# Last-query value product of two head pairs on 64-column halves of TensorE, with one division for both, in a fused attention and gated-MLP kernel

## The chip, the cores and the metric

The kernel runs on one core of one Trainium2 chip. The metric is device time in microseconds (us). Three runs gave 441.95, 442.55 and 442.66 us; the median is 442.55 us.

The engines of the core are named as the profile names them: PE is TensorE's matmul side, PEld its weight load side, DVE is VectorE, ACT is ScalarE, POOL is GpSimd and SP is the queue that issues most of the DMAs. PSUM is the memory that TensorE writes its products to, SBUF the memory that it reads from.

## What is computed

A threshold attention feeds a gated MLP with a spatial mixing step. Batch 8, 8 heads, 576 positions, head dimension 64.

```python
scores = (q @ k.T) / 8                        # per batch and head, 576 x 576
keep   = scores >= rowmax(scores) - tau       # tau = 0.02
attn   = where(keep, exp(scores - rowmax), 0); attn /= attn.sum(-1)
x      = concat_heads(attn @ v)               # 8 x 576 x 512
h = relu(x @ w_in); u, v = halves(h)          # 512 columns each
v = layernorm(v); v = w_spatial @ v + b_spatial
out = (u * v) @ w_out
```

The part that the change touches is `attn @ v`, with its division by the row sum, for the last 64 of the 576 queries of each head.

## The kernel before, in words

**Tiles.** Heads are handled as 32 pairs (`NPAIR`), four pairs to a batch. A pair's 576 queries are four chunks of 128 (chunk c of `steps`, c from 0 to 3) and a rest of 64. The rests of two neighbouring pairs, 2m and 2m+1, are put together into one chunk of 128 rows (chunk 4): rows 0 to 63 are those of pair 2m, rows 64 to 127 those of pair 2m+1. A step computes the scores of one chunk for both heads of the pair (L712, 64x64 tiles of TensorE), the row maxima (L746 on DVE), the exponentials (L761 or L764 on ACT, then L776 on DVE or L781 on ACT) and leaves bf16 numerators.

**The transposed numerators.** For the value product the numerators must lie with keys on the partitions and queries on the free axis. They are transposed by DMA (`turn_p`, L787; `turn_rest`, L799) or, for some rests, by TensorE (`pr_pe`). For the rests of pairs 2m and 2m+1 the result is a tile `ptr` of 128 x 9 x 128: nine blocks of 128 keys, and in each block 128 query columns, of which the first 64 belong to pair 2m and the last 64 to pair 2m+1. Blocks 0 to 3 are the first head's keys, blocks 5 to 8 the second head's, block 4 holds the last 64 keys of both heads.

**The value product.** `weigh` (L390) makes the product of one such tile with one pair's values. It issues nine matmuls: one with block 4 and 130 moving columns (L392; 2 heads x (64 values + 1 column of ones)), and eight with 65 moving columns (L397). The stationary side is always a full 128-column block of the transposed tile, and the column of ones makes the row sum come out as column 64 of each head. `pv` (L411) calls `weigh` for two chunks of one pair, `pv_rest` (L446) calls it for the two pairs that share a rest tile: pair 2m's values with all 128 query columns into PSUM columns 0 to 129, then pair 2m+1's values with all 128 query columns into columns 130 to 259. Of the first product only partitions 0 to 63 are used, of the second only 64 to 127; the other half of each is computed and never read.

**The division.** `divide` (L400) takes the reciprocals of the row sums of a PSUM tile (L404: 128 x 4 values) and multiplies (L406). For `pv` that is one multiplication of 128 x 256. For `pv_rest` it is two, of 64 x 128 each: the partitions of each pair with that pair's columns. The result goes to `xn`, block 8.

**What sets the order.** Every engine's instructions are issued in the order that the strings `ORDER` (L16 to L82) spell out by hand, one token for each small task; the same string serves every batch from the fourth on. `R0` and `R1` are the matmuls of `pv_rest` for the two rest tiles of a batch, `r0` and `r1` their divisions; both of a batch's rests come after its chunk 4 scores, `R1` in the following batch's string. `P`/`p` are `pv`, `S`/`Y` scores (L712), `M` maxima (L746), `QR` (L357) and `QA`/`QB` (L338) the f32 transposes of queries and keys, `u` (L610 and, for its last part, L615), `v`, `s` (L639) and `o` (L668) the MLP. After the strings, the last rest's product is issued by hand among the last MLP tasks (L1079).

**Buffers that bind neighbours.** Products other than scores go through `bank()` (L291), which has only two PSUM banks (`ps_f`, `bufs=2`) until the last stretch. A task's matmuls can start only when the division or copy of the task two banks earlier has been done. Scores have two buffers of their own.

**64-column stationary tiles** occur in the kernel already: `ends` (L526) puts two products into partitions 0 to 63 and 64 to 127 of one bank with 64 stationary columns each (L530, L533), alternating between them. In the profile their shape is written 128*64; full blocks are 128*128 and the scores 64*64.

Of the kernel before, what the change touches and what calls it, by code (L numbers as in the profile page):

```python
# [11 lines left out]
ALU = mybir.AluOpType  # L12
# [75 lines left out]
def kernel(  # L88
# [17 lines left out]
    nc = tc.nc  # L106
# [6 lines left out]
    P = 128  # L113
# [29 lines left out]
    v_ring = [const.tile([P, 10, D + 1], BF16, name=f"v{i}") for i in range(4)]  # L143
# [147 lines left out]
    def bank(dtype=F32, n=512):  # L291
        if wide:

            turn[0] += 1
            if turn[0] % 8 not in (2, 3):
                return wide[0].tile([P, n], dtype, name="t")
        return ps_f.tile([P, n], dtype, name="f")
# [5 lines left out]
    qks, pts, xns, xts = {}, {}, {}, {}  # L303
# [83 lines left out]
            turn(tm, P * (c - 1), 0, c)  # L387
        nc.scalar.mul(out=qkt[:, 0, 192:576], in_=tm[:, 0:384], mul=scale)

    def weigh(t, at, pt, vt):  # L390

        nc.tensor.matmul(out=t[:, at:at + 130], lhsT=pt[:, 4, :],  # L392
                         rhs=vt[:, 4:6, :].rearrange("p b d -> p (b d)"),
                         start=True, stop=False)
        for h in range(2):
            for j in range(4):
                nc.tensor.matmul(out=t[:, at + 65 * h:at + 65 * h + 65], lhsT=pt[:, 5 * h + j, :],  # L397
                                 rhs=vt[:, 6 * h + j, :], start=False, stop=(h == 1 and j == 3))

    def divide(t, parts):  # L400

        o = t[:, 0:260].rearrange("p (g d) -> p g d", d=65)
        r = small.tile([P, 4], F32, name="r")
        nc.vector.reciprocal(out=r, in_=o[:, :, 64])  # L404
        for ps, g0, g1, dst in parts:
            nc.vector.tensor_tensor(  # L406
                out=dst, in0=o[ps, g0:g1, 0:64],
                in1=r[ps, g0:g1].unsqueeze(2).broadcast_to([ps.stop - ps.start, g1 - g0, 64]),
                op=ALU.mult)

    def pv(i, part):  # L411

        b, hp = divmod(i, HP)
        hold = {}

        def mm():
            t = hold["t"] = bank()
            for k in range(2):
                weigh(t, 130 * k, pts[i, part][:, k], v_ring[i % 4])

        def ev():
            xn = x_nat(i // 2)
            at = 4 * (i % 2) + 2 * part
            divide(hold["t"], [(slice(0, P), 0, 4,
                                xn[:, at:at + 2, :].rearrange("p c (h d) -> p (c h) d", h=2))])
        return "dve", mm, ev

    def xt_of(b):
# [5 lines left out]
    def x_nat(m):  # L434

        if m not in xns:
            xns[m] = xp.tile([P, 9, P], BF16, name="xn")
        return xns[m]
# [7 lines left out]
    def pv_rest(m):  # L446

        hold = {}

        def mm():  # L450
            t = hold["t"] = bank()
            for k in range(2):
                weigh(t, 130 * k, pts[m], v_ring[(2 * m + k) % 4])

        def ev():
            xn = x_nat(m)[:, 8, :]
            divide(hold["t"], [(slice(64 * k, 64 * k + 64), 2 * k, 2 * k + 2,
                                xn[64 * k:64 * k + 64].rearrange("p (h d) -> p h d", h=2))
                               for k in range(2)])
        return "dve", mm, ev  # L460

    def x_of(b, f, cols):
# [225 lines left out]
        return "act", mm, ev, send  # L688


    halves = [slice(64 * k, 64 * k + 64) for k in range(2)]
    at = (96, 864)

    def on_act(g):
# [322 lines left out]
    with tc.manual_schedule():  # L1017
# [18 lines left out]
        for _ in range(7):  # L1036
            nc.tensor.matmul(out=ps_f.tile([P, 512], F32, name="f").rearrange(
                "p (a b) -> p a b", a=4), lhsT=warm,
                rhs=warm.unsqueeze(1).broadcast_to([P, 4, P]), start=True, stop=True)
# [84 lines left out]
```

## Time and profile before

| what | value |
|---|---|
| median of three runs | 442.55 us |
| lowest and highest run | 441.95 and 442.66 us |
| profiled execution, first to last instruction (span) | 440.2 us |
| median run less that span (what lies around it) | 2.35 us |
| instructions of the program | 12827 |
| mean granted TensorE clock | 0.999 |
| busy in the batch from 242.5 to 293.0 us: PE, DVE, ACT, POOL | 49.74, 47.10, 47.73, 21.71 of 50.50 us |
| waits of DVE for scores, whole span | 9.3 us (22 times) and 8.5 us (16 times) |
| `pv_rest` in the span | 16 times, 18 matmuls and 3 DVE instructions each |

How to read it: the page gives a busy time for each engine, a chain of work that is followed back from the last instruction, and groups of instructions with their mean durations. Matmuls overlap, so 49.74 us of PE busy time do not mean that TensorE had no room left; the distance from the start of one matmul to the start of the next is what a product really occupies. A table by stage shows the batches from 192 us to 394 us to be nearly equal, 50.5 us each. In a timeline row, the first number is the start and the second the length of a run of like instructions.

### The profile page before, as it was taken

The numbers are of one execution on the slowest core, as the hardware profiler recorded it, in microseconds if no ns is written. First come the engines' busy times: TensorE is split into PE (matmuls) and PEld (weight loads), VectorE is DVE, ScalarE is ACT, GpSimd is POOL, SyncE is SP. The second block draws the span as 40 slices with busy tenths as digits, with TensorE's granted clock in tenths as the row PEclk, the third lists the DMA queues.
The fourth block names the chain that finished last, engine by engine and source line by source line (L and its number), as shares of the span: only waits on it lengthen the run. The fifth ranks groups of instructions, "written<-read, shape, count | busy, mean of one in ns | idle before, by whom it ended". The sixth has DMA issues, their size and how long they took to land.

```text
span 440.2 us, 12827 instructions
## 1 busy us (share of the span) xinstructions
PE 411.0 (93%) x4997; PEld 260.9 (59%) x5048; DVE 394.3 (90%) x641; ACT 388.0 (88%) x621; POOL 178.7 (41%) x383
## 2 busy tenths in 40 slices
PE   8677789999999999999999999999999999999995
PEld 4454556566555666666565666666566666565553
DVE  6997899998999898999999998999989998999782
ACT  3899799999899999999999989999899999999352
POOL 1445443860416511773146711574127711345021
PEclk9999999999999999999999999999999999999999
DMA  7999999899999999999999999999999998976913
GB/s 197 284 213 215 286 224 240 176 180 208 247 157 246 189 188 193 223 220 187 234 216 166 246 216 200 221 231 182 218 188 221 235 190 158 163 111 83 281 67 109
DMA packets 222620, 88.15 MB, mean 200 GB/s; under 512 B 193632, under 2 KB 218336, under 8 KB 222560
## 3 DMA queue, kind: packets, MB, share of 16 engines
q1 hardware_dynamic: 222032, 86.48, 95.0%
q8 instruction: 40, 0.66, 0.6%
q0 software_dynamic: 160, 0.52, 0.3%
q10 hardware_dynamic: 368, 0.33, 0.2%
q14 instruction: 20, 0.16, 0.1%
HBM read 32.79 MB, written 9.44 MB: 96 GB/s over the span
## 4 chain that ended last, share of the span: by engine, by line
DVE 36%; PE 35%; ACT 18%; issue 8%; DMA 1%; POOL 0%; POOLq 0%; DVEq 0%; ACTq 0%
PE s L712 14%; DVE s L746 13%; DVE p L776 9%; DVE negm L746 6%; ACT e L761 6%; ACT e L764 4%; ACT p L781 4%; PE f L610 3%; PE f L668 3%; PE f L397 2%; PE f L639 2%; DVE xn L406 2%; PE f L338 2%; DVE st L565 2%; PE f L545 2%
## 5 line engine op out<-in xcount | busy, mean ns | idle before, releaser
L712 PE MATMUL s<-qkT 64*64 64x160 f32 (+1 forms) x2304 | 171.8, 415 | 13.5 <-ACT e L761 7.3
L712 PEld LDWEIGHTS s<-qkT 64*64 64x64 f32 x2304 | 106.7, 132 | 68.4 <-ACT e L761 17.4
L761 ACT ACTIVATE e<-s,negm 128x576 f32<-128x576 f32 x168 | 117.2, 744 | 12.1 <-DVE negm L752 6.5
L746 DVE TENSOR_REDUCE s<-s 128x2 f32<-128x1152 f32 (+1 forms) x91 | 115.3, 1268 | 10.8 <-PE s L712 9.3
L764 ACT ACTIVATE e<-s,negm 128x576 f32<-128x576 f32 x120 | 84.8, 749 | 9.4 <-DVE negm L746 8.1
L746 DVE TENSOR_REDUCE negm<-s 128x2 f32<-128x1152 f32 (+1 forms) x62 | 81.2, 1313 | 8.8 <-PE s L712 8.5
L776 DVE SCALAR_TENSOR_TENSOR p<-e,ctau 128x1152 bf16<-128x1152 f32 x60 | 85.5, 1427 | 1.3 <-ACT e L764 1.2
L781 ACT ACTIVATE p<-e 128x1152 bf16<-128x1152 f32 x68 | 79.0, 1171 | 0.4
L197 POOL COPY qn<-ql 128x512 f32<-128x512 f32 x31 | 25.5, 821 | 81.1 <-PE s L712 80.7
L397 PE MATMUL f<-v,pT 128*128 128x65 bf16 x1008 | 44.5, 194 | 0.0
L397 PEld LDWEIGHTS <-pT 128*128 128x128 bf16 x1024 | 41.4, 97 | 3.5 <-issue 1.8
L350 POOL COPY qkT<-qkT 64x64 f32<-64x64 f32 x32 | 7.9, 247 | 85.3 <-PE s L712 42.4
L406 DVE TENSOR_TENSOR xn<-f,r 128x256 bf16<-128x256 f32 (+1 forms) x93 | 35.4, 380 | 2.9
L639 PE MATMUL f<-wsT,vn 128*128 128x512 bf16 x117 | 32.6, 380 | 1.4 <-ACT qkT L320 0.4
L610 PE MATMUL f<-xT,w_in 128*128 128x512 bf16 x111 | 29.4, 381 | 0.5
L392 PE MATMUL f<-v,pT 128*128 128x130 bf16 x126 | 27.7, 220 | 1.1 <-DVE xT L314 0.7
L595 POOL TENSOR_SCALAR vn<-vrel,rs,nm 128x512 bf16<-128x512 f32 (+1 forms) x35 | 27.0, 770 | 3.6
L320 ACT COPY qkT<-f 128x512 f32<-128x512 f32 (+1 forms) x56 | 24.5, 439 | 3.4 <-PE f L357 3.2
L545 PE MATMUL f<-w_in,xT 128*128 128x512 bf16 x99 | 26.8, 379 | 0.8
L668 PE MATMUL f<-w_o,gT 128*128 128x512 bf16 x92 | 24.2, 380 | 0.4
L224 POOL CAST v<-vl 128x512 bf16<-128x512 f32 x32 | 20.0, 625 | 10.3 <-PE s L712 9.4
L230 POOL CAST v<-vx 64x64 bf16<-64x64 f32 x64 | 20.8, 326 | 1.9
(166 smaller groups left out, 570.9 us busy)
## 6 DMA issues: line engine op xcount, KB each, us to landing
vl<-in_v_dram SPq DMA_DIRECT2D x16, 512.0 KB, 4.7
ql<-in_q_dram SPq DMA_DIRECT2D x15, 512.0 KB, 5.0
kl<-in_k_dram SPq DMA_DIRECT2D x15, 512.0 KB, 5.3
out_dram<-oo SPq DMA_DIRECT2D x12, 512.0 KB, 5.0
uT<-in_moe_w_in_dram SPq DMA_DIRECT2D x3, 512.0 KB, 4.8
uT<-in_moe_w_spatial_dram SPq DMA_DIRECT2D x2, 576.0 KB, 4.6
pT<-p SPq DMA_TRANSPOSE x65, 6.3
vx<-in_v_dram SPq DMA_DIRECT2D x16, 64.0 KB, 3.7
```

The costliest lines, as they stand in the source:

```text
L397: nc.tensor.matmul(out=t[:, at + 65 * h:at + 65 * h + 65], lhsT=pt[:, 5 * h + j, :], rhs=vt[:, 6 * h + j, :], start=False, stop=(h == 1 an ...
L406: nc.vector.tensor_tensor(out=dst, in0=o[ps, g0:g1, 0:64], in1=r[ps, g0:g1].unsqueeze(2).broadcast_to([ps.stop - ps.start, g1 - g0, 64]), ...
L545: nc.tensor.matmul(out=t, lhsT=x_of(b, f, slice(c * P, (c + 1) * P)), rhs=w_in[:, f, 512:1024], start=(f == 0), stop=(f == 3))
L610: nc.tensor.matmul(out=t, lhsT=w_in[:, m, f * P:(f + 1) * P], rhs=x_of(b, m, slice(0, 512)), start=(m == 0), stop=(m == 3))
L639: nc.tensor.matmul(out=t, lhsT=vn[:, c, f * P:(f + 1) * P], rhs=wsT[:, c, 0:512], start=(c == 0), stop=(c == 4))
L668: nc.tensor.matmul(out=t[:n], lhsT=gs[b][:, f, c * P:c * P + n], rhs=w_o[:, f, :], start=(f == 0), stop=(f == 3))
L712: made.append(nc.tensor.matmul(out=s_ring[g % 2][halves[k], at[h] + lo:at[h] + hi], lhsT=qks[n][halves[h], 0, m:m + 64], rhs=qks[n][halves ...
L746: nc.vector.tensor_reduce(out=nm[:, heads], in_=view(s_ring[g % 2], at[h0], dims), axis=AX.X, op=ALU.max, negate=True)
L761: nc.scalar.activation(out=e, in_=s, func=ACT.Prelu, bias=bias_, scale=scale if steps[g][1] == 4 else 1.0, alpha=1e30)
L764: nc.scalar.activation(out=e, in_=s, func=ACT.Exp, bias=bias_)
L776: nc.vector.scalar_tensor_tensor(out=numerators(g), in0=ef, scalar=ctau, in1=ef, op0=ALU.is_ge, op1=ALU.mult)
L781: nc.scalar.activation(out=numerators(g), in_=e_ring[g % 3].rearrange("p h s -> p (h s)"), func=ACT.Exp)
```

## The change

`weigh` gets a parameter `rows`, by default all 128. It selects the stationary columns of the transposed tile and the partitions of the PSUM tile. `pv_rest` passes columns 0 to 63 for pair 2m and 64 to 127 for pair 2m+1, and both write to the same PSUM columns, 0 to 129. The four groups of 65 columns become two, and one division of 128 x 128 serves both pairs in place of two of 64 x 128. `pv` computes what it did.

```diff
-    def weigh(t, at, pt, vt):
-        nc.tensor.matmul(out=t[:, at:at + 130], lhsT=pt[:, 4, :],
+    halves = [slice(64 * k, 64 * k + 64) for k in range(2)]
+    def weigh(t, at, pt, vt, rows=slice(0, P)):
+        t = t[rows]
+        nc.tensor.matmul(out=t[:, at:at + 130], lhsT=pt[:, 4, rows],
                          rhs=vt[:, 4:6, :].rearrange("p b d -> p (b d)"),
                          start=True, stop=False)
         for h in range(2):
             for j in range(4):
-                nc.tensor.matmul(out=t[:, at + 65 * h:at + 65 * h + 65], lhsT=pt[:, 5 * h + j, :],
-                                 rhs=vt[:, 6 * h + j, :], start=False, stop=(h == 1 and j == 3))
-    def divide(t, parts):
-        o = t[:, 0:260].rearrange("p (g d) -> p g d", d=65)
+                nc.tensor.matmul(out=t[:, at + 65 * h:at + 65 * h + 65],
+                                 lhsT=pt[:, 5 * h + j, rows], rhs=vt[:, 6 * h + j, :],
+                                 start=False, stop=(h == 1 and j == 3))
+    def divide(t, n, dst):
+        o = t[:, 0:65 * n].rearrange("p (g d) -> p g d", d=65)
         r = small.tile([P, 4], F32, name="r")
-        nc.vector.reciprocal(out=r, in_=o[:, :, 64])
-        for ps, g0, g1, dst in parts:
-            nc.vector.tensor_tensor(
-                out=dst, in0=o[ps, g0:g1, 0:64],
-                in1=r[ps, g0:g1].unsqueeze(2).broadcast_to([ps.stop - ps.start, g1 - g0, 64]),
-                op=ALU.mult)
+        nc.vector.reciprocal(out=r[:, 0:n], in_=o[:, :, 64])
+        nc.vector.tensor_tensor(out=dst, in0=o[:, :, 0:64],
+                                in1=r[:, 0:n].unsqueeze(2).broadcast_to([P, n, 64]), op=ALU.mult)
...
     def pv_rest(m):
...
             for k in range(2):
-                weigh(t, 130 * k, pts[m], v_ring[(2 * m + k) % 4])
+                weigh(t, 0, pts[m], v_ring[(2 * m + k) % 4], halves[k])
         def ev():
-            xn = x_nat(m)[:, 8, :]
-            divide(hold["t"], [(slice(64 * k, 64 * k + 64), 2 * k, 2 * k + 2,
-                                xn[64 * k:64 * k + 64].rearrange("p (h d) -> p h d", h=2))
-                               for k in range(2)])
+            divide(hold["t"], 2, x_nat(m)[:, 8, :].rearrange("p (h d) -> p h d", h=2))
```

The `ORDER` strings, the number of matmuls and what each waits for in the source stay as they are.

More of the change, by code (lines that the diff above doesn't have):

```diff
@@ L423, in ev @@
             at = 4 * (i % 2) + 2 * part
-            divide(hold["t"], [(slice(0, P), 0, 4,
-                                xn[:, at:at + 2, :].rearrange("p c (h d) -> p (c h) d", h=2))])
+            divide(hold["t"], 4, xn[:, at:at + 2, :].rearrange("p c (h d) -> p (c h) d", h=2))
         return "dve", mm, ev
@@ L688, in moe_o @@
         return "act", mm, ev, send
-    halves = [slice(64 * k, 64 * k + 64) for k in range(2)]
     at = (96, 864)
```

## The prediction

> **What bounds the kernel.** I read the page's busy times first, then its chain of work that ended last.
>
> ```profile
> PE 411.0 (93%) x4997; PEld 260.9 (59%) x5048; DVE 394.3 (90%) x641; ACT 388.0 (88%) x621; POOL 178.7 (41%) x383
> DVE 36%; PE 35%; ACT 18%; issue 8%; DMA 1%; POOL 0%; POOLq 0%; DVEq 0%; ACTq 0%
> ```
>
> Three engines are nearly full and the chain changes hands between DVE, PE and ACT. So a saving counts only in the places where its engine is the late one. The change touches 16 places; I went through each. The groups kept apart by shape give the prices.
>
> ```profile
> L397 PE MATMUL f<-v,ptr 128*128 128x65 bf16 x240 | 10.9, 194 | 0.0
> L404 DVE RECIPROCAL r<-f 128x4 f32<-128x4 f32 x78 | 13.4, 172 | 1.2 <-PE f L397 1.1
> L406 DVE TENSOR_TENSOR xn<-f,r 64x128 bf16<-64x128 f32 x30 | 8.7, 289 | 0.7
> L406 DVE TENSOR_TENSOR xn<-f,r 128x256 bf16<-128x256 f32 x63 | 26.7, 424 | 2.2
> L565 DVE BATCH_NORM_STATS2 st<-vrel 128x6 f32<-128x512 f32 x12 | 8.1, 679 | 0.0
> L565 DVE BATCH_NORM_STATS2 st<-vrel 64x6 f32<-64x512 f32 x7 | 4.8, 683 | 0.2
> L615 PEld LDWEIGHTS <-w_in 128*128 128x128 bf16 x128 | 4.3, 98 | 2.9 <-DVE xn L406 2.7
> ```
>
> **DVE, removed.** Each of the 16 rests loses one L406 of 64x128. The chain row at 244.11 below comes 0.30 us after the one at 243.81, so one costs 0.30 us with its issue. The one that stays grows from 64 to 128 partitions. L565 costs the same on 64 as on 128 partitions (683 and 679 ns), so I take 289 ns for it. The bounds are 283 ns, the shortest 64x128 one, and 424 ns, the 128x256 row; with 424 the saving would be 0.17 us. I take 0.30. The reciprocal falls from 4 to 2 values: L752, of 128x2, takes 156 ns against 172, so at most 0.02 us, counted as nothing. Total off DVE: 16 x 0.30 = 4.8 us.
>
> **PE, the 18 products of a rest.** Their number and moving columns stay; only the stationary columns fall from 128 to 64. Now a run of eight L397 and the following L392 lie 0.25 us apart, 32 ns a product. The trace has no 64-column tile with so short a product. From below: 29 ns, the spacing of the 16 L615 products (64 moving columns); or, since L530 and L533 on different column halves start 4 ns apart, an overlap, but here all nine of pair 2m come before pair 2m+1's, so only one product in 18 can gain, 0.03 us. From above: load and product one after the other. These rows give the load:
>
> ```profile
> 85.41 0.10 PEld L397 LDWEIGHTS <-pT 128*128 128x128 bf16 x1
> 85.56 0.14 PEld L530 LDWEIGHTS <-xT 128*64 128x64 bf16 x2
> ...
> 87.69 0.11 PEld L610 LDWEIGHTS <-w_in 128*128 128x128 bf16 x2 [0.23 <-issue]
> ```
>
> Two 64-column loads take 0.14 us where one takes 0.11, so they follow at 29 ns; two 128-column ones follow at about 15. The narrow load is the slower one, but still within 32 ns, and L530's second load starts while its first product streams. I take 32 ns as now, with an upper end of 29 + 32 = 61 ns.
>
> The Trainium skill speaks against this: "TensorEngine Tiling (Array Packing)", Restrictions, says that column tiling disables the fast weight load, and "TensorE: Matmul & The Clock Gate", LDWEIGHTS, prices a plain load at columns / 1.2, for 64 columns 53 ns. An estimate by that: some 21 ns more for each of 18 products, 0.38 us a rest, and some 444.8 us in place of the sum below. The 29 ns between L530's loads speak for the slower kind of load, at about half that price.
>
> **PE, switches of tile shape.** This is the cost that the source doesn't show.
>
> ```profile
> 245.48 0.41 PE L397 MATMUL f<-v,pT 128*128 128x65 bf16 x8
> 245.73 0.22 PE L392 MATMUL f<-v,pT 128*128 128x130 bf16 x1
> 245.79 0.41 PE L397 MATMUL f<-v,pT 128*128 128x65 bf16 x8
> 246.13 1.20 PE L712 MATMUL s<-qkT 64*64 64x160 f32 x16
> 247.48 0.64 PE L615 MATMUL f<-xT,w_in 128*128 128x64 bf16 x16
> ```
>
> From a run of eight L397 to a product of the same shape it is 0.25 us, to L712 with its 64*64 tiles 0.34: a switch costs 0.09 us. Into 128*64 the same comes out (L819 at 419.78 to L530 at 420.08 is 0.30, less the 0.215 between L819 products), and out of it too (L533 at 188.98 to L610 at 189.29). The first product after entering is 0.024 us longer (L530 at 420.08, next at 420.32, later ones 0.215 apart). A rest between two 128*128 tasks gets two new switches, between a 128*128 and a 64*64 task one, between two L712 none. Counting neighbours in the timeline: six rests with two (66.14, 191.66, 242.19, 292.76, 343.33, 412.48 us), nine with one, one with none (393.63): 21 switches, 1.95 us, and 0.4 us of first products. No semaphore wait is added, but a switch is a stall: queued behind it on PE are the next transposes or scores, and DVE's maxima wait for those.
>
> **Place by place. First rest of a steady batch** (191.66, 242.19, 292.76, 343.33). The chain in order of time:
>
> ```profile
> 243.81 0.28 DVE xn L406
> 244.11 0.29 DVE xn L406
> ...
> 247.00 0.44 DVE xn L406
> 247.43 0.05 issue
> 247.48 0.64 PE f L615 x16
> ```
>
> Both L406 are on it. DVE then runs without a pause to the next pair's division (247.00), and PE's L615 waits for that division's bank. PE could have gone earlier: elsewhere a task follows a run of 16 L712 after 1.13 us (252.69 to 253.82), and 246.13 + 1.13 = 247.26, against 247.48. Here the new switches are covered: the rest waits for its bank until ACT ends L316 (242.13), which is past the end of the entering switch (241.92 + 0.11 + 0.09), and the next L338 (242.98) waits for ACT's L320, which ends at 242.93, past 242.77 + 0.03 + 0.09. So DVE comes 0.30 earlier, L615 becomes ready at 247.18 and starts at 247.26: 0.22. The L610 behind it waited for a second division, 0.07 us past the spacing, and that goes as well, so by 247.76 PE is 0.27 ahead. From there the chain is dense PE work to 257.4. 4 x 0.27 = 1.08 us. If the cover fails, PE's 0.22 us eat the gain.
>
> **Second rest of a steady batch** (161.85, 212.39, 262.96, 313.53, 364.10): nothing. The chain runs through ACT from 263.98 to 268.86 (its L761 and L781 without a gap), beside this rest. PE gets one switch and one first product, 0.12 us; the L712 at 268.90, which waits for ACT, could have started at 268.36 + 0.34 = 268.70, so 0.20 us cover it.
>
> **The others.** At 90.23 both divisions are on the chain and L615 at 92.05 waits for the rest's own bank, PE idle 0.42 us: gain 0.30. At 393.63 the chain is DVE up to 398.59, then ACT, whose L764 could start only 0.1 us sooner unless its earlier wait shrinks too: between 0.1 and 0.3, I take 0.20. At 29.24 and 66.14 PE waits for ACT (0.81 us at 32.12, 0.21 us at 67.74) and the division is off the chain: nothing. At 119.65 (chain on PE) one switch and a first product cost 0.11; at 139.05, where a wait for a bank covers most, 0.03. The last, at 412.48, has the chain on PE and DVE waiting for it:
>
> ```profile
> 413.30 0.18 DVE L404 RECIPROCAL r<-t 128x4 f32<-128x4 f32 x1 [0.80 <-PE t L397]
> ```
>
> Two switches and first products there: 0.22 us lost.
>
> **Sum.** 1.08 + 0.30 + 0.20 - 0.11 - 0.03 - 0.22 = 1.22 us, about a quarter of what DVE is spared. The span goes from 440.2 to 439.0. The median of the runs is 2.35 us above the span, for which nothing changes: 442.55 - 1.22 = 441.3 us. A measurement of this kernel tells about 0.2% (0.9 us) from no change, so this forecast is just beyond it.
>
> **Rivals.**
> - *Waits change hands.* The 0.27 us of a steady batch is handed to ACT or to a bank wait before the batch ends (ACT's first L764 after the rest can come only 0.15 us sooner, since its L576 ends at 246.76). Then 0.5 gained and 0.36 lost: 442.4. For it: chain shares of 36, 35 and 18%.
> - *The switches are PE's time* (slower). If TensorE has no room where I see 0.1 to 0.2 us, all 21 switches and first products count, 1.95 + 0.4 = 2.3 us, and DVE only waits longer for scores: 443.9 to 444.9. It decides from about 0.2 us more PE time in a second rest, the slack at 268.90. For it: DVE already waits 9.3 + 8.5 us for L712. Against it: PE's waits for bank or ACT or slack, at 13 of the 16 places.
> - *The 64-column loads aren't hidden* (61 ns a product). 0.5 us more a rest. First rests: 0.03 of slack at 242.98 and 0.11 at the L712 of 243.62 (it waits for ACT) leave 0.36, so L615 starts at 247.62, 0.14 late; second rests lose 0.12 + 0.5 - 0.2 = 0.42; the three on PE's chain 0.5 more each: 0.56 + 2.1 + 1.86 - 0.5 = 4.0, so 446.5. At 43 ns a product (0.2 us more a rest) first rests still gain 0.24, second ones lose 0.1, the chain's three 0.9 together: the sum is nothing.
> - *DVE's saving passes in full*: 442.55 - 4.8 + 0.4 = 438.1; something between, 439 to 440, if second rests gain too. Against it: ACT's unbroken row there.
>
> **Chances.** Forecast 0.52, waits change hands 0.17, switches 0.17, loads 0.08, saving in full or half 0.06. A sixth of the forecast's own spread lies within 0.2%. Faster by over 0.2%: 0.44 + 0.06 = 0.50; within: 0.08 + 0.15 = 0.23; slower: 0.17 + 0.08 + 0.02 = 0.27. The range reaches from 440.2, which leaves out the full saving, to 444.4, which leaves out the loads and part of the switches.
>
> **What would show it.** Right: L406 of 128x128 near 289 ns, 16 of them; DVE busy down by about 4.8 us; L392 and L397 on ptr as 128*64, a run of 18 still about 0.59 us; L615 after a first rest no longer waiting for xn, and the batch 0.27 us shorter. Wrong: products 40 ns apart or more; L338 after a rest moved beyond 242.98 relative to ACT; more DVE waiting for L712; ACT waiting longer near 263.98.

## The result and the profile after

The changed kernel takes 439.79 us (median of 13 runs, 438.06 to 442.64), the kernel before 443.02 us on the same chip (13 runs, 441.86 to 444.66). The ratio is 0.9935 with a 95% interval of 0.9914 to 0.9957: 2.9 us faster (1.9 to 3.8). The forecast was 1.2 us. The direction was right, the size was less than half, and the time lies below the range.

The two profiled executions show less than the runs: the span falls from 440.2 to 439.1 us, by 1.1, as if the forecast had been right. That is a coincidence, as the next part shows. The page of the changed kernel, busy times and chain:

```profile
PE 410.4 (93%) x4997; PEld 260.2 (59%) x5048; DVE 388.2 (88%) x625; ACT 385.9 (88%) x621; POOL 179.8 (41%) x383
PE 52%; DVE 19%; ACT 18%; DMA 5%; issue 5%; POOL 0%; POOLq 0%; DVEq 0%; ACTq 0%; SPq 0%
```

DVE is busy 6.1 us less: 16 multiplications at 289 ns are 4.6 of it. The durations of all its rows together fall by 4.8 us; the other 1.3 is overlap of neighbouring rows, which the busy time counts once. Its share of the chain falls from 36 to 19%, PE's rises from 35 to 52%: the chain of the changed kernel runs through TensorE over about half of its length. The groups by shape answer to the prices of the prediction:

```profile
L400 PE MATMUL f<-v,ptr 128*64 128x65 bf16 x240 | 9.5, 195 | 0.0
L400 PEld LDWEIGHTS <-ptr 128*64 128x64 bf16 x256 | 9.2, 111 | 0.3 <-issue 0.3
L408 DVE RECIPROCAL r<-f 128x2 f32<-128x2 f32 x15 | 2.4, 160 | 0.0
L409 DVE TENSOR_TENSOR xn<-f,r 128x128 bf16<-128x128 f32 x15 | 4.4, 292 | 0.5
L612 PEld LDWEIGHTS <-w_in 128*128 128x128 bf16 x128 | 4.3, 98 | 1.6 <-DVE r L408 1.1 <-DVE xn L409 0.2
```

The one multiplication (L409, before L406) takes 292 ns (289 forecast). The wait of the last `u` products (L612, before L615) for DVE falls from 2.7 to 1.3 us. What is left is mostly 0.23 us a time (a row of `no_recip` below shows one), and there L612 follows the scores after 1.13 us, the distance that the prediction found at a place without a wait: no division is waited for any more, whatever the row names.

**Where the time went.** I compared the start of each instruction in the two traces, from one place to the next. From 60 us to the end the changed kernel gains 3.44 us. Between 28 and 60 us it loses 2.85, and by 28 us it is some 0.5 ahead, which makes up the 1.1 of the spans. Nearly all of the loss is at one place:

```profile
52.36 0.23 PE L395 MATMUL f<-v,pT 128*128 128x130 bf16 x1 [3.30 <-DMA pT<-p]
```

PE stands for 3.30 us there, until a DMA transpose has landed. It was in flight for 7.39 us; the same one took 5.65 us before, where PE stood for 0.66 us at this place. So there are two questions: why the gain after 60 us is nearly three times the forecast, and whether the change causes the loss before it.

### The profile page after: what moved, and what is told of

It is laid out like the page before. It is cut to its first block, busy times and chain, and to the rows that moved or that the text cites. A ratio compares the mean times of both kernels' runs of the same rounds, so it can differ in the third digit from the quotient of the medians.

```text
span 439.1 us, 12815 instructions
## 1 busy us (share of the span) xinstructions
PE 410.4 (93%) x4997; PEld 260.2 (59%) x5048; DVE 388.2 (88%) x625; ACT 385.9 (88%) x621; POOL 179.8 (41%) x383
## 4 chain that ended last, share of the span: by engine, by line
PE 52%; DVE 19%; ACT 18%; DMA 5%; issue 5%; POOL 0%; POOLq 0%; DVEq 0%; ACTq 0%; SPq 0%
PE s L708 22%; PE f L636 6%; DVE p L772 5%; DVE s L742 5%; ACT e L757 5%; PE f L400 5%; DVE negm L742 5%; ACT e L760 4%; DMA pT<-p 4%; PE f L338 4%; PE f L665 4%; PE f L607 3%; ACT p L777 2%; PE f L395 2%; PE f L542 1%
## 5 line engine op out<-in xcount | busy, mean ns | idle before, releaser
L400 PE MATMUL f<-v,pT 128*128 128x65 bf16 x1008 | 44.5, 194 | 0.0
L400 PEld LDWEIGHTS <-pT 128*128 128x128 bf16 x1024 | 41.5, 98 | 2.5 <-issue 0.4
L409 DVE TENSOR_TENSOR xn<-f,r 128x256 bf16<-128x256 f32 (+1 forms) x78 | 31.1, 399 | 2.7
L395 PE MATMUL f<-v,pT 128*128 128x130 bf16 x126 | 27.8, 220 | 3.8 <-DMA pT<-p 3.5
```

The costliest lines, as they stand in the source:

```text
L395: nc.tensor.matmul(out=t[:, at:at + 130], lhsT=pt[:, 4, rows], rhs=vt[:, 4:6, :].rearrange("p b d -> p (b d)"), start=True, stop=False)
```

## The experiments

The theory, A: the shorter division moves more instructions than the prediction counted (about 0.43 us at each first rest of a steady batch, 0.14 at each second one), the halves cost PE about nothing, and the late landing is chance that meets either kernel. The distance between the first rests of neighbouring batches, 50.57 us before and 50.00 after, is the clearest gauge, since it holds none of the first 60 us.

**The changed kernel again, `again`.**

> The changed kernel once more, for the spread and for the place at 50 us where its profiled run waited 3.30 us for a transposed tile (DMA pT<-p) that the kernel before did not wait for. Theory A (the wait is the chance of one run, the change itself gives about 3.6 us by the shifts at the sixteen places): a ratio of 0.990 to 0.994, and in this profile no such wait or a shorter one, with a span of 436 to 438 us. Rival B (the change moves the early transposes so that they land late, and pays for it every time): the wait of about 3 us at 52 us is there again, span about 439 us.

It took 438.85 us (6 runs) against 442.72 (23 runs), ratio 0.9899 (0.9867 to 0.9930). The profile repeats both findings: 3.45 us gained from 60 us on, and a wait of 2.71 us for the same transpose at 52.14 us. Two out of two speak for the rival that the change causes the late landing. The next profiles test that.

**The kernel before, profiled again, `before_a` and `before_b`** (no edit).

> The kernel before, profiled again, to see whether it too waits for a transposed tile near 50 us in some executions. Theory A (that wait is the chance of one execution, in both kernels: the fastest runs of the two are 441.7 and 438.1 us, 3.6 us apart, and both kernels have runs 4 us above their fastest): in one of two profiles a wait of PE for DMA pT<-p of over 0.5 us between 35 and 60 us, with a span over 441 us; a profile without it has a span near 440.2. Rival B (only the kernels with the shorter division wait, since 4 of 4 of their profiles did and 2 of 2 of the others did not): no such wait in either. In both, steady batches of 50.57 us.

> As before_a, one more profile of the kernel before. Theory A: one of the two shows the wait for DMA pT<-p. Rival B: neither does.

They took 444.38 and 443.89 us, with spans of 442.6 and 442.1 against the 440.2 of the first profile. POOL's timeline, first of the profile that the prediction was made from, then of `before_a`:

```profile
41.75 0.61 POOL L197 COPY kn<-kl 128x512 f32<-128x512 f32 x1 [0.42 <-DMA kl<-in_k_dram]
```

```profile
44.17 0.61 POOL L197 COPY kn<-kl 128x512 f32<-128x512 f32 x1 [3.36 <-DMA kl<-in_k_dram]
```

The kernel before also loses 2.9 and 2.6 us between 28 and 60 us in two of its three profiles, but for a load of keys, not for the transpose that the expectation named. Measured against the first profile of before, the loss in that stretch runs from 0.1 less than none (`again_2`, below) to 2.9 us in the 14 profiles of this case. So late transfers there belong to both kernels, and the profile of before was a lucky one and that of after an unlucky one. For the transpose alone this is not shown: it was in flight for 7.1 to 7.4 us in three of the seven profiles with the shorter division at every rest (`after`, `again`, `dve_only`), and for 5.5 to 6.0 us in the four others and in all seven profiles of the remaining kernels. Three are too few to tell chance from an effect of the change. What sets when a transfer lands late stays open. The fastest runs, where chance should weigh least, are 3.8, 3.6 and 3.5 us apart in the three comparisons with this many runs (441.86 and 438.06, 441.74 and 438.12, 441.80 and 438.29), near the 3.4 us.

**Division alone, `dve_only`:** the kernel before, with one multiplication of 128 x 128. It takes the rows of every second pair from the first pair's columns, so it leaves out their result.

```diff
-            divide(hold["t"], [(slice(64 * k, 64 * k + 64), 2 * k, 2 * k + 2,
-                                xn[64 * k:64 * k + 64].rearrange("p (h d) -> p h d", h=2))
-                               for k in range(2)])
+            divide(hold["t"], [(slice(0, P), 0, 2, xn.rearrange("p (h d) -> p h d", h=2))])
```

> Only DVE's side of the change: the products stay as before (128 stationary columns, 128*128), and the rest gets one multiplication of 128 x 128 in place of two of 64 x 128. It leaves out the last rows of every second pair, which are taken from the first pair's columns. Theory A (DVE's 0.30 us per rest, passed on through the waits for banks, is all of the gain; PE's switches are covered or paid back by the overlap of the two halves): within 0.4 us of the changed kernel, ratio 0.990 to 0.995, steady batches of 49.9 to 50.1 us against 50.57 before. Rival C (the overlap of the two 64-column halves on PE brings a part of the gain): 1 us or more slower than the changed kernel, steady batches of 50.2 us or more.

440.87 us (12 runs), ratio 0.9927 (0.9903 to 0.9951). The steady batch is 50.00 us, exactly that of the whole change: the division gives all of the steady gain. Its fastest run (438.09) equals that of `again` (438.12), its median is 2.0 us above. Its profile lost 1.3 us between 28 and 60 us and another 1.1 near 356, both with PE waiting for transposes (2.56 and 0.97 us); whether chance alone makes the median higher stays open.

**Half columns alone, `halves_only`:** the changed kernel, but with two multiplications of 64 partitions.

```diff
-            divide(hold["t"], 2, x_nat(m)[:, 8, :].rearrange("p (h d) -> p h d", h=2))
+            xn = x_nat(m)[:, 8, :]
+            o = hold["t"][:, 0:130].rearrange("p (g d) -> p g d", d=65)
+            r = small.tile([P, 4], F32, name="r")
+            nc.vector.reciprocal(out=r[:, 0:2], in_=o[:, :, 64])
+            for ps in halves:
+                nc.vector.tensor_tensor(
+                    out=xn[ps].rearrange("p (h d) -> p h d", h=2), in0=o[ps, :, 0:64],
+                    in1=r[ps, 0:2].unsqueeze(2).broadcast_to([64, 2, 64]), op=ALU.mult)
```

> Only PE's side of the change: 64-column products into the partitions of each pair, but still two multiplications of 64 x 128, so that DVE has as many instructions as before. Everything is computed. Theory A: no gain, ratio 0.999 to 1.002, steady batches of 50.5 to 50.7 us; the switches show where PE is the late engine, 0.1 to 0.2 us at the last rest. Rival C: a gain of 0.5 us or more, ratio below 0.998.

442.99 us (12 runs), ratio 1.0007 (0.9984 to 1.0029), steady batch 50.55 us. The 21 switches of tile shape, 2.3 us in the forecast's worst case, cost nothing that the runs can tell. The trace puts them at 0.3 us from 60 us on: at the rests on PE's chain it shows +0.28 (119 to 131 us) and +0.15 us (the last one).

**Both pairs' products in turn, `interleaved`:** the changed kernel with the two halves alternating.

```diff
-            for k in range(2):
-                weigh(t, 0, pts[m], v_ring[(2 * m + k) % 4], halves[k])
+            both = [(k, t[halves[k]], v_ring[(2 * m + k) % 4]) for k in range(2)]
+            for k, o, vt in both:
+                nc.tensor.matmul(out=o[:, 0:130], lhsT=pts[m][:, 4, halves[k]],
...
+            for h in range(2):
+                for j in range(4):
+                    for k, o, vt in both:
+                        nc.tensor.matmul(out=o[:, 65 * h:65 * h + 65],
...
```

> The changed kernel with the products of the two pairs alternating, so that each product runs beside one of the other column half: the run of 18 should shrink from about 0.52 us to about 0.30 us. Theory A (a steady batch is limited elsewhere at both rests: the first rest's successor waits for ACT to free its bank, the second lies beside ACT's chain): only the three rests on PE's chain gain, about 0.2 us each, so 0.3 to 0.7 us below the changed kernel, steady batches the same within 0.05 us. Rival D (PE holds 52% of the chain after the change, so its time counts at every rest): 16 x 0.22 = 3.5 us below the changed kernel, steady batches 0.4 us shorter.

438.69 us (6 runs), ratio 0.9893 (0.9859 to 0.9927). A run of 18 now takes 0.306 us from the first start to the last, yet the steady batch stays at 50.00 us; from 60 us on it gains 3.95 us where the changed kernel gains 3.45. So the steady rests are not held by PE's products, and the few on PE's chain are.

**One of the two rests only, `first_only` and `second_only`:** the change for the pairs with `m % 2 == 0`, or with `m % 2 == 1`; the others do as before.

```diff
+        new = m % 2 == 0
...
-                weigh(t, 0, pts[m], v_ring[(2 * m + k) % 4], halves[k])
+                weigh(t, 0 if new else 130 * k, pts[m], v_ring[(2 * m + k) % 4],
+                      halves[k] if new else slice(0, P))
```

> The change for the first rest of each batch alone; the second rest keeps 128-column products and two multiplications. The changed kernel's steady batch is 50.00 us against 50.57, of which the comparison of the two traces puts 0.43 to the first rest and 0.15 to the second. If these two are separate gains (each passes through waits of its own): steady batches of 50.13 to 50.16 us. If the second rest only gains because the first one has made DVE early: 50.0 us here.

> The change for the second rest of each batch alone. If ACT's row beside it is unbroken, as the prediction had it: steady batches of 50.57 us. If ACT's L761 after the two L781 had been waiting for DVE's maximum (L752) and not for ACT itself: 50.42 us, and that L761 0.13 us closer to the L781 before it.

`first_only`: 440.28 us (one run), steady batches 50.13, 50.38 and 50.13 us. `second_only`: 441.86 us (one run), 50.41, 50.80 and 50.44 us. In two batches of three the first is 0.44 shorter than before and the second 0.13 to 0.16, which sum to the whole 0.57: separate gains.

The third batch of each, and the totals, need a word. From 60 us on `first_only` gains 1.72 us and `second_only` 0.09, together 1.8 of the 3.45. In both kernels DVE stands idle for 0.30 to 0.37 us longer than before at about 172 and about 245 us. One of these rows, in `first_only`, had no idle time before the change and waits for nothing that the profile shows:

```profile
245.19 1.36 DVE L756 TENSOR_REDUCE negm<-s 128x2 f32<-128x1152 f32 x1 [0.30 <-issue]
```

At 67 us `first_only` also loses 0.30 us to a late transpose. Without these five stops the two would gain about 3.5 us together, so the gains still add up; why DVE stops there, with no counterpart in the traces of before or of the whole change, stays open.

The gain of the second rest is the one that the prediction put at nothing, because of ACT's "unbroken row". ACT's timeline before and in `second_only` (its L791 and L771 are L781 and L761):

```profile
265.24 2.21 ACT L781 ACTIVATE p<-e 128x1152 bf16<-128x1152 f32 x2
267.47 1.37 ACT L761 ACTIVATE e<-s,negm 128x576 f32<-128x576 f32 x2
```

```profile
265.33 2.21 ACT L791 ACTIVATE p<-e 128x1152 bf16<-128x1152 f32 x2
267.44 1.37 ACT L771 ACTIVATE e<-s,negm 128x576 f32<-128x576 f32 x2
```

The first row ends at 267.45 in the trace of before and the next begins at 267.47: no gap to see. In `second_only` the next begins 0.10 us before the first ends: the distance between the starts is 2.11 instead of 2.23 us. So ACT could have started 0.12 us earlier, and was waiting for the maxima of this DVE row of before, which ends at 267.38:

```profile
267.23 0.15 DVE L752 TENSOR_SCALAR negm<-s 128x2 f32<-128x2 f32 x1
```

The trace of before held the sign of it. The row ahead of the L781 there ends at 265.35, 0.11 us after they begin:

```profile
263.98 1.37 ACT L761 ACTIVATE e<-s,negm 128x576 f32<-128x576 f32 x2 [0.76 <-DVE negm L752]
```

**One more multiplication, `third_mul`:** the kernel before, with the second multiplication of each rest made twice.

```diff
-                               for k in range(2)])
+                               for k in (0, 1, 1)])
```

> The kernel before with a third multiplication of 64 x 128 at every rest, a repetition of the second into the same place, so DVE gets 0.30 us more per rest and nothing else changes. Theory A (at both rests of a steady batch DVE was already the late one, so what is added there passes in full): steady batches of 51.1 to 51.2 us (50.57 + 2 x 0.30). Rival E (the gain of the change came from the slack of one particular wait, and the other way the waits absorb it, as for a quarter of DVE's time): 50.7 to 50.85 us.

446.79 us (one run) against 442.84 (18 runs). The steady batches grow from 50.57 to 51.20 and 51.23 us: 0.63 to 0.66 for two multiplications of 0.30 each. A third one is 51.49, with 0.26 us more near 306 us that I did not trace. From 60 us on the loss is 4.6 us. More DVE work passes to the time in full at both rests.

**Still less on DVE, `no_recip`:** the changed kernel with a copy in place of the multiplication and no reciprocal.

```diff
-            divide(hold["t"], 2, x_nat(m)[:, 8, :].rearrange("p (h d) -> p h d", h=2))
+            o = hold["t"][:, 0:130].rearrange("p (g d) -> p g d", d=65)
+            nc.vector.tensor_copy(out=x_nat(m)[:, 8, :].rearrange("p (h d) -> p h d", h=2),
+                                  in_=o[:, :, 0:64])
```

> The changed kernel without the reciprocal at the rests: the 128 x 128 multiplication becomes a copy of the same shape, and the division of the last queries is left out. DVE loses another 0.2 us per rest. Theory A (after the change the next limits are PE before L615 and ACT's row of L777, so nothing is left to be had from DVE there): steady batches of 49.93 to 50.0 us. Rival F (DVE is still the late one at both rests): 49.6 us.

It leaves out the division of these rows. 440.44 us (one run), steady batch 50.00 us, no shorter; from 60 us on it gains 3.1 us, no more than the changed kernel. The wait ahead of L612 (L614 in this kernel) is the 0.23 us of the changed kernel, against 0.44 before and 0.45 in `third_mul`:

```profile
247.57 0.52 PEld L614 LDWEIGHTS <-w_in 128*128 128x128 bf16 x16 [0.23 <-DVE r L408]
```

The lever is used up: with one multiplication gone the batch is PE's.

**Interleaved and changed kernel side by side, `interleaved_2` and `again_2`** (no new edit).

> The alternating products again, beside the changed kernel on the same chip. From the first comparison: steady batches of 50.00 us as the changed kernel, and 0.2 to 0.5 us less in all, from the rests on PE's chain. If that was the spread of the runs: no difference within 0.2 us.

> The changed kernel on the same chip as the alternating one, for their difference. Theory A (compute gains 3.6 us, late transfers in the first 60 us come by chance in either kernel): ratio 0.989 to 0.994, fastest run near 438.1 us.

`interleaved_2`: 439.56 us (7 runs), ratio 0.9926 (0.9894 to 0.9959). `again_2`: 440.07 us (12 runs), ratio 0.9935 (0.9906 to 0.9964). From 60 us on they gain 3.86 and 3.46 us. The traces put the interleaved version 0.4 to 0.5 us ahead, twice, at the same places; the runs, whose intervals overlap, don't separate the two. It has the lowest time of the kernels that compute everything, 437.67 us in one run, and is faster than the kernel before in both comparisons.

PE's timeline of `again_2` and of `interleaved_2` at a first rest (L454 and L460 are its 130 and 65 column products):

```profile
242.09 0.23 PE L395 MATMUL f<-v,ptr 128*64 128x130 bf16 x1
242.16 0.32 PE L400 MATMUL f<-v,ptr 128*64 128x65 bf16 x5
242.29 0.24 PE L395 MATMUL f<-v,ptr 128*64 128x130 bf16 x1
242.32 0.47 PE L400 MATMUL f<-v,ptr 128*64 128x65 bf16 x11
```

```profile
240.57 0.25 PE L454 MATMUL f<-v,ptr 128*64 128x130 bf16 x2
240.64 0.43 PE L460 MATMUL f<-v,ptr 128*64 128x65 bf16 x16
```

In `again_2` the second L395, which begins the other pair's half, starts after five L400; the first pair has eight. So the second half begins while three products of the first are still to come. From the first start to the last the run of 18 takes 0.51 to 0.52 us where 32 ns a product and one longer first one gave 0.59. That repays 0.07 us, nearly a whole switch.

## Why the prediction was wrong, point by point

**DVE's saving: right.** One rest gives DVE 0.30 us (the extra multiplication of `third_mul` shows the same from the other side), and the reciprocal next to nothing.

**Price of the 64-column products: right.** The spacing is 32 ns. The Trainium skill's "TensorE: Matmul & The Clock Gate", LDWEIGHTS, would have put a load of 64 columns at 53 ns; the trace has products with such loads 32 ns apart, so that price did not show here.

**Switches of tile shape: right in size, wrong in what they sum to.** A switch takes 0.09 us. But the step "only one product in 18 can gain, 0.03 us" failed: three products overlap. At the three rests on PE's chain the forecast had a loss of 0.11 + 0.03 + 0.22 = 0.36 us; the traces show a gain of 0.11 and of 0.05 at the first two and a loss of 0.12 to 0.17 at the last: together 0.37 us better. Not all of that is the overlap: 0.12 of it is an exponential (L761 at 129.89) that waited for DVE, as at the second rests below.

**First rest of a steady batch: right mechanism, undersized.** Forecast 0.27, measured 0.40 to 0.45. Both terms came as forecast: the distance from L712 to L615 fell from 1.35 to 1.13 us (0.22), that from L615 to the next L610 from 0.55 to 0.48 (0.07). The step that failed is "From there the chain is dense PE work": it was not. The next `pv` had to wait for its bank too, as PE's and DVE's timelines of before show:

```profile
249.02 0.22 PE L392 MATMUL f<-v,pT 128*128 128x130 bf16 x1
```

```profile
248.55 0.41 DVE L310 TENSOR_SCALAR uT<-f 128x256 bf16<-128x256 f32 x1
```

L310 ends at 248.96, the product starts at 249.02, 0.99 us after its neighbour's start at 248.03. In the changed kernel that distance is 0.86 us: 0.13 more. A further 0.05 lies ahead of `pv`'s first product (L338 to L392, 1.83 us before, 1.78 after), and some 0.03 is given back in between: 0.44. With 0.43 as the middle of the four, 4 x 0.16 = 0.64 us were missed.

**Second rest of a steady batch: the step that failed outright.** "nothing. The chain runs through ACT [...] (its L761 and L781 without a gap)". Five times 0.14 to 0.15, 0.72 us. The recorded end of an ACT row lies about 0.1 us past the point at which the next can start, so rows that touch are rows with a small wait.

**At 393.63: the same mistake.** Forecast 0.20, measured 0.55. The row of before names the wrong engine, and the DVE row says why (ACT's and DVE's timelines):

```profile
396.42 1.37 ACT L761 ACTIVATE e<-s,negm 128x576 f32<-128x576 f32 x2 [0.61 <-PE s L712]
```

```profile
396.15 0.16 DVE L752 TENSOR_SCALAR negm<-s 128x2 f32<-128x2 f32 x1
```

The exponential also needs the negated maxima of L752, which end at 396.31 just ahead of it. That wait shrank by 0.43 us, and a second one by 0.12.

**The others.** At 90.23: 0.30 forecast, 0.33 measured. At 66.14 "nothing" was 0.22: a bank freed earlier moved a maximum at 71 us (L746), which I had not followed beyond PE's wait for ACT at the rest itself. At 29.24 the chance of the first 60 us hides any effect.

**The sum.** 1.22 forecast, and 0.64 + 0.72 + 0.35 (393.63) + 0.22 + 0.37 + 0.03 = 2.33 missed: 3.55 us, against the 3.44 to 3.46 of the three traces of the changed kernel. The rival "something between, 439 to 440, if second rests gain too" was what happened; I gave it and the full saving 6% together.

**One execution each.** Reading the kernel from one span was a second weakness: the profile of before was among its early finishes (440.2 us, then 442.6 and 442.1). It is not what broke the forecast, since its terms lie after 60 us, where the three profiles of before agree within 0.07 us; but it made the comparison of the two spans (1.1 us) look like a confirmation. The 2.35 us between span and median come from the same mix: a run's time lies about 1.8 us above its own span (440.91 and 439.1 us for the changed kernel), and the table set the span of a fast execution against the median of three.

## What to carry to other kernels

Where engines hand a chain to each other, follow a saved instruction through every bank and buffer that it frees, until a distance between two starts equals one that is seen elsewhere without a wait; a single overlooked wait can cost half of the answer. Rows that touch are no proof of a busy engine: compare the distance of their starts with that of a place where nothing can be waited for. And take two or three profiles of one kernel before a microsecond of span is read as an effect.

## What the runs showed that I had not expected

- **Column halves overtake.** With 64-column tiles a half that was issued later starts while three of the earlier half's products are to come, and 18 products take 0.51 us in sequence and 0.306 us in turn, from the first start to the last (17 ns each, in place of 32). The Trainium skill's "TensorE: Matmul & The Clock Gate", The mechanism, says that matmuls start strictly in the order of issue; the recorded starts at 242.29 and 242.32 disagree, for products on different column halves.
- **ACT's rows overlap by 0.1 us**, 2.11 us from the start of a pair of instructions to the start of the next row, for a pair recorded as 2.21 long.
- **The same program's transfers land up to 3 us apart** between 28 and 60 us, from one execution to the next. Of the six profiles that were 0.2 to 0.7 us early at 28 us, five lost 1.2 to 2.9 us in that stretch and one lost 0.1; of the other seven, set against the first profile of before, two lost 1.3 and 1.6 us and five next to nothing. I didn't find the cause.
